# Two 8-byte tiles moved to the right end of SBUF in an FFT filter kernel with a bilinear layer

## The chip, the core and the metric

The kernel runs on one core of a Trainium2 chip. The metric is the device time of one execution in microseconds (us). The core has a matrix engine (TensorE, PE in the profile; PEld is its weight load), VectorE (DVE), ScalarE (ACT), GpSimd (POOL), and queues that issue DMAs (SP's and ACT's are used here). SBUF is the working memory, 128 partitions wide; every tile lies at one byte offset that is the same in all its partitions.

## The reference

```python
X = np.fft.rfft(x, axis=1)                     # x: (8, 3072, 256) float32
Y = X * (filt_r + 1j * filt_i)[None, :, :]     # 1537 x 256 filter
y = np.fft.irfft(Y, n=3072, axis=1).reshape(8 * 3072, 256)
out = ((y @ w_a) * (y @ w_b)) @ w_out          # 256 -> 1536 -> 256, float32 out
```

The weights w_a, w_b and w_out come as float64.

## The kernel before

The transform of length 3072 is done as two stages of matrix products, 128 by 24, forward and inverse (`s1`, `s2`, `is1`, `is2`), with the filter multiplied in between. The bilinear layer follows on each group of 512 rows: `pair` computes two of the twelve column blocks of `y @ w_a` and `y @ w_b` by a seven-product scheme (`term`, lines 582 to 584), multiplies them on VectorE, and `project` (lines 601 to 603) multiplies by `w_out`. Each float32 operand is split in a rounded high part and a low part (`xoh` and `xol`, `gh` and `gl`, `wah` and `wal`, ...), and each product is made of three fp32r matmuls.

Batch 0 is transformed first by functions of its own (`first_s1`, `first_s2`, `first_is1`), in plain float32. During that time and the start of batch 0's layer the float64 weights are converted on VectorE, ScalarE and GpSimd (`conv_...`). From then on the layer of batch b and the transform of batch b + 1 are interleaved by hand: `plan` and `early` hold lists of steps for each slot, and `pair` calls them. The order of instructions on every engine is the order in which the code is written (`manual_schedule`).

SBUF is given out by pools. Those on the left grow upwards in the order `const`, `p2`, then `pw` for the conversion, which is closed and replaced by `later`. Those on the right grow downwards from the end: `fr` for batch 0's transform, which is closed and replaced by `moe`. Each tile takes a multiple of 32 bytes per partition. The offsets of the program before, in bytes, follow from the sizes:

- `const` begins at 1,152. Its first nine tiles (`wah`, `wal`, `wbh`, `wbl`, `woh`, `wol`, `fct`, `flt`, `ict`) have sizes that are multiples of 128, so all nine begin at multiples of 128. `sct` follows at 115,456. It has 8 bytes and takes 32.
- All that lies behind `sct` on the left therefore begins 32 past a multiple of 128: `filt0` to `filt3` and `nyq` in `const`, `xoh`, `xol`, `tt` and `gt` in `p2`, all tiles of `later` (`xt`, `st`, `xh`, `xl`, `zh`, `zl`, `y`, `v`, `yh`, `yl`, `zt`, `t`), and in `pw` `fcf` and `icf`.
- `cut`, again 8 bytes, lies in `pw` behind `icf`; the tiles of `pw` behind it (`raw`, `e`, `m`, `s`) begin 64 past a multiple of 128.
- The right end is at 229,344, which is 96 past a multiple of 128, and all tiles of `fr` and `moe` have sizes that are multiples of 128. So all of them (`x0`, `zf`, `z0`, `xi`; `xf`, `cs`, `g`, `gh`, `gl`, `s`, `ot`, ...) begin 96 past one.

`sct` holds two scale factors for each partition. One DMA (line 699) loads it at 24.6 us, and VectorE reads it in `s2` and `cross` of batches 1 to 7. `cut` holds two constants; two VectorE memsets write it (lines 681 and 682), and the two ScalarE activations of `conv_scale` (lines 260 and 261) read it as their bias.

Of the kernel before, what the change touches and what calls it, by code (L numbers as in the profile page):

```python
# [9 lines left out]
F32 = mybir.dt.float32  # L10
# [186 lines left out]
def fft_filter_bilinear_kernel(ctx: ExitStack, tc, x, filt, fny, wa, wb, wo, s1c, gc, fc, fl, ic, sc, s1f, ff, fi, out):  # L197
# [3 lines left out]
    def pool(name, bufs=1, space=None):  # L201
        kw = {} if space is None else {"space": space}
        return ctx.enter_context(tc.tile_pool(name=name, bufs=bufs, **kw))

    const = pool("const")
    p2 = pool("p2", 2)


    first, front = ExitStack(), ExitStack()
    pw = first.enter_context(tc.tile_pool(name="pw", bufs=1))  # L210
    fr = front.enter_context(tc.tile_pool(name="fr", bufs=2, side="right"))
# [20 lines left out]
    fct = const.tile([128, 3, 128], F32R, name="fct")  # L232
    flt = const.tile([96, 2, 128], F32R, name="flt")
    ict = const.tile([128, 3, 96], F32R, name="ict")
    sct = const.tile([128, 2], F32, name="sct")
    fcf = pw.tile([96, 2, 128], F32, name="fcf")
    icf = pw.tile([128, 2, 96], F32, name="icf")
    cut = pw.tile([128, 2], F32, name="cut")
    filts = [const.tile([128, 2, D], F32, name=f"filt{i}") for i in range(NFT)]
    nyq = const.tile([128, D], F32, name="nyq")  # L240

# [600 lines left out]
```

## Time and profile before

| | before |
|---|---|
| median of 3 runs | 2661.09 us (2660.5 to 2661.87) |
| the profiled execution: its own time | 2662.36 us |
| its span, first to last instruction | 2660.6 us |
| PE busy | 2589.5 us, 97% of the span |
| DVE, ACT, POOL busy | 63%, 53%, 50% |
| granted TensorE clock, mean | 0.985 |
| moved by DMA | 310.88 MB, 117 GB/s over the span |

A share of busy time is a mean over stages. Here there are three: about 200 us in which batch 0 is transformed and the weights are converted, then a steady part to about 2600 us, and an end of some 60 us. "PE busy" counts an instant when at least one matmul is in flight; a matmul's own duration (280 ns) is longer than the distance from one to the next, because they are pipelined.

### The profile page before, as it was taken

The page shows a single profiled execution, that of the slowest core. Times are in us where ns is not written, and L with a number is a line of the kernel's source. Part 1 is how long each engine was busy: PE and PEld are TensorE (multiplying, and loading weights), DVE is VectorE, ACT ScalarE, POOL GpSimd, SP SyncE. Part 2 cuts the span into 40 slices and gives each one's busy share as a digit, 9 for nine tenths or more (in the row PEclk, how much of TensorE's full clock was granted, in tenths as well). Part 3 has the DMA queues.
Part 4 walks back from the last instruction along what each step waited for, and adds up shares of the span by engine and source line. Part 5 has one row for each costly group of instructions (what it writes and reads, how often), then busy time and mean ns, then how long its engine had stood idle before and what let it go on. Part 6 is the DMA issues. An engine that isn't in the chain of part 4 may idle for free.

```text
span 2660.6 us, 54030 instructions
## 1 busy us (share of the span) xinstructions
PE 2589.5 (97%) x20920; PEld 2518.2 (95%) x20920; DVE 1665.2 (63%) x2648; ACT 1412.2 (53%) x2630; POOL 1321.8 (50%) x1044
## 2 busy tenths in 40 slices
PE   5789999999999999999999999999999999999999
PEld 2389999999999999999999999999999999999998
DVE  5775785558845687456865478545884468744443
ACT  3456555555555555555555555555555555545444
POOL 3575454545545555454545545454454545434333
PEclk6899999999999999999999999999999999999999
DMA  7626441344324443244423454234432444311000
GB/s 248 181 98 223 141 135 62 127 150 137 113 74 136 158 137 97 78 163 136 145 66 112 139 154 139 66 119 156 132 120 66 144 152 141 94 33 33 29 21 17
DMA packets 213634, 310.88 MB, mean 117 GB/s; under 512 B 21393, under 2 KB 121298, under 8 KB 213330
## 3 DMA queue, kind: packets, MB, share of 16 engines
q1 hardware_dynamic: 184882, 278.85, 32.7%
q10 hardware_dynamic: 28496, 28.58, 3.5%
q8 instruction: 164, 2.69, 0.4%
q14 instruction: 92, 0.75, 0.1%
HBM read 202.49 MB, written 108.00 MB: 117 GB/s over the span
## 4 chain that ended last, share of the span: by engine, by line
PE 88%; POOL 4%; DVE 3%; issue 2%; DMA 2%; ACT 1%; SPq 0%; ACTq 0%; POOLq 0%; DVEq 0%
PE po L603 10%; PE ps_p L582 10%; PE ps_p L583 9%; PE ps_p L584 9%; PE po L601 9%; PE po L602 9%; PE ps_r L584 5%; PE ps_r L582 5%; PE ps_r L583 5%; PE ps L548 3%; PE ps_q L582 2%; PE ps_q L584 2%; PE ps_q L583 2%; PE ps L361 2%; POOL xol L567 2%
## 5 line engine op out<-in xcount | busy, mean ns | idle before, releaser
L591 POOL TENSOR_TENSOR gl<-g,gh 128x512 fp32r<-128x512 f32 x576 | 747.1, 1297 | 959.2 <-ACT gh L590 894.7
L601 PE MATMUL po<-woh,gh 128*128 128x256 f32 x2304 | 656.1, 285 | 0.0
L603 PE MATMUL po<-woh,gl 128*128 128x256 f32 x2304 | 649.7, 282 | 3.1 <-POOL gl L591 1.1
L590 ACT CAST gh<-g 128x512 fp32r<-128x512 f32 x576 | 358.9, 623 | 550.6 <-DVE g L649 532.0
L602 PE MATMUL po<-wol,gh 128*128 128x256 f32 x2304 | 645.9, 280 | 0.0
L627 DVE TENSOR_TENSOR cs<-ps_r,s 128x512 f32<-128x512 f32 x288 | 199.1, 691 | 450.6 <-PE ps_r L584 397.0
L623 ACT COPY s<-ps_p 128x512 f32<-128x512 f32 x576 | 338.0, 587 | 242.5 <-PE ps_p L584 205.9
L603 PEld LDWEIGHTS po<-woh,gl 128*128 128x128 f32 x2304 | 433.8, 188 | 7.8 <-POOL gl L591 7.8
L601 PEld LDWEIGHTS po<-woh,gh 128*128 128x128 f32 x2304 | 434.9, 189 | 3.1
L602 PEld LDWEIGHTS po<-wol,gh 128*128 128x128 f32 x2304 | 434.7, 189 | 2.9
L582 PE MATMUL ps_p<-xoh,wah 128*128 128x256 f32 x1152 | 326.0, 283 | 12.0 <-DVE cs L627 7.6
L584 PE MATMUL ps_p<-xol,wbh 128*128 128x256 f32 x1152 | 323.9, 281 | 0.0
L583 PE MATMUL ps_p<-xoh,wal 128*128 128x256 f32 x1152 | 323.6, 281 | 0.0
L584 PE MATMUL ps_p<-xol,wah 128*128 128x256 f32 x1152 | 323.1, 280 | 0.0
L582 PE MATMUL ps_p<-xoh,wbh 128*128 128x256 f32 x1152 | 322.7, 280 | 0.0
L583 PE MATMUL ps_p<-xoh,wbl 128*128 128x256 f32 x1152 | 322.6, 280 | 0.0
L627 DVE TENSOR_TENSOR cs<-ps_q,s 128x512 f32<-128x512 f32 x288 | 199.1, 691 | 187.0 <-PE ps_q L584 161.4
L649 DVE TENSOR_TENSOR g<-cs 128x512 f32<-128x512 f32 x288 | 300.9, 1045 | 6.1 <-POOL gl L591 6.1
L567 POOL TENSOR_TENSOR xol<-xf,xoh 128x256 fp32r<-128x256 f32 x192 | 246.9, 1307 | 20.9 <-ACT xoh L566 20.9
L661 DVE TENSOR_TENSOR g<-ps_p,cs 128x256 f32<-128x256 f32 x288 | 122.1, 424 | 213.2 <-ACT cs L660 210.2
L442 POOL TENSOR_TENSOR yl<-y,yh 128x512 fp32r<-128x512 f32 x112 | 144.3, 1289 | 223.7 <-ACT yh L441 223.7
L582 PEld LDWEIGHTS ps_p<-xoh,wah 128*128 128x128 f32 x1152 | 217.5, 189 | 13.8 <-DVE cs L627 8.5
(125 smaller groups left out, 6239.1 us busy)
## 6 DMA issues: line engine op xcount, KB each, us to landing
filt<-in_filt SPq DMA_DIRECT2D x336, 128.0 KB, 2.8
z<-zh SPq DMA_DIRECT2D x112, 256.0 KB, 3.0
zt<-z SPq DMA_DIRECT2D x112, 256.0 KB, 3.0
td<-t ACTq DMA_DIRECT2D x128, 192.0 KB, 2.2
out<-ot SPq DMA_DIRECT2D x95, 256.0 KB, 2.1
tt<-td SPq DMA_DIRECT2D x47, 512.0 KB, 4.2
xt<-in_x SPq DMA_DIRECT2D x84, 256.0 KB, 2.9
st<-s1d SPq DMA_DIRECT2D x84, 256.0 KB, 3.4
```

Of the source, the lines that this page charges most:

```text
L567: nc.gpsimd.tensor_tensor(out=xl[:, o], in0=xf[:, i], in1=f32(xh[:, o]), op=ALU.subtract)
L582: nc.tensor.matmul(o, wh[:, p, w], xh[:, i], start=first and h == 0, stop=False, skip_group_check=True)
L583: nc.tensor.matmul(o, wl[:, p, w], xh[:, i], start=False, stop=False, skip_group_check=True)
L584: nc.tensor.matmul(o, wh[:, p, w], xl[:, i], start=False, stop=True, skip_group_check=True)
L590: nc.scalar.copy(out=gh, in_=g[:, f])
L591: nc.gpsimd.tensor_tensor(out=gl, in0=g[:, f], in1=f32(gh), op=ALU.subtract)
L601: nc.tensor.matmul(o, gh[:, ts], woh[:, n], start=n == 0 and j % 2 == 0, stop=False, skip_group_check=True)
L602: nc.tensor.matmul(o, gh[:, ts], wol[:, n], start=False, stop=False, skip_group_check=True)
L603: nc.tensor.matmul(o, gl[:, ts], woh[:, n], start=False, stop=n == NF - 1, skip_group_check=True)
L623: nc.scalar.copy(out=s, in_=bank)
L627: nc.vector.tensor_tensor(out=cs[:, :, n], in0=bank, in1=s, op=ALU.add)
L649: nc.vector.tensor_tensor(out=g[:, 0].rearrange("p (t n) -> p t n", t=2), in0=cs[:, 0, 0:2], in1=cs[:, 1, 0:2], op=ALU.mult)
```

## The change

A new pool `edge` is opened on the right, ahead of `fr`. It holds one tile `few` of 24 float32 numbers per partition (96 bytes). `sct` becomes its columns 0 and 1, `cut` its columns 2 and 3; the other 20 columns are not used. The two old tiles go. No instruction is added, removed or moved; what changes is the offset at which tiles lie.

```diff
+    edge = ctx.enter_context(tc.tile_pool(name="edge", bufs=1, side="right"))
+    few = edge.tile([128, 24], F32, name="few")
+    sct, cut = few[:, 0:2], few[:, 2:4]
...
     ict = const.tile([128, 3, 96], F32R, name="ict")
-    sct = const.tile([128, 2], F32, name="sct")
     fcf = pw.tile([96, 2, 128], F32, name="fcf")
     icf = pw.tile([128, 2, 96], F32, name="icf")
-    cut = pw.tile([128, 2], F32, name="cut")
     filts = [const.tile([128, 2, D], F32, name=f"filt{i}") for i in range(NFT)]
```

With `few` at 229,248, the right-hand tiles move down by 96 bytes. On the left, what lay behind `sct` moves down by 32, and what lay behind `cut` in `pw` by 64. All of them then begin at multiples of 128.

## Rows read from the trace of the kernel before

**Rows 1.** Busy time by stretch: start:end, length, then each engine, clock, DMA share, GB/s
```profile
0.00:100.00 100.00, 61.36 (x126) 29.62 (x126) 67.86 (x121) 44.02 (x79) 46.28 (x46) 0.74 0.75 241
100.00:200.00 100.00, 78.29 (x478) 66.59 (x479) 68.16 (x117) 49.83 (x99) 61.55 (x54) 0.86 0.34 111
...
300.00:700.00 400.00, 398.99 (x3281) 392.83 (x3279) 272.41 (x414) 217.17 (x403) 202.85 (x158) 1.00 0.40 126
...
1900.00:2300.00 400.00, 399.22 (x3287) 393.43 (x3287) 272.22 (x417) 217.42 (x405) 200.21 (x155) 1.00 0.40 126
...
2600.00:2661.00 61.00, 54.53 (x459) 53.92 (x457) 22.94 (x41) 23.48 (x44) 19.27 (x15) 0.98 0.05 18
```

**Rows 2.** Who waited for whom, 220 to 2600 us: total, times, longest
```profile
PEld po L603 <- POOL gl L591: 6.3, 21, 0.3
...
PEld ps_r L584 <- POOL xol L567: 3.9, 7, 0.6
```

**Rows 3.** Chain that ended last, 0 to 220 us: start, length, what
```profile
3.06 6.72 DMA raw<-in_wa
...
13.53 5.83 DMA z<-z
20.05 4.21 DMA z<-z
...
28.27 5.82 DMA z<-z
...
48.51 6.49 DMA raw<-in_wo
```

**Rows 4.** TensorE's matmuls one by one: start, duration, line, tiles
```profile
1505.42 0.28 PE L601 MATMUL po<-woh,gh 128*128 128x256 f32 x1
...
1506.84 0.28 PE L582 MATMUL ps_p<-xoh,wah 128*128 128x256 f32 x1
...
1507.56 0.28 PE L361 MATMUL ps<-xh,st 128*128 128x256 f32 x1
...
1508.27 0.28 PE L601 MATMUL po<-woh,gh 128*128 128x256 f32 x1
...
1508.98 0.28 PE L582 MATMUL ps_p<-xoh,wah 128*128 128x256 f32 x1
...
1511.79 0.28 PE L601 MATMUL po<-woh,gh 128*128 128x256 f32 x1
...
1512.50 0.28 PE L582 MATMUL ps_r<-xoh,wah 128*128 128x256 f32 x1
```

**Rows 5.** Groups by line and shape on TensorE, 300 to 2500 us
```profile
L603 PE MATMUL po<-woh,gl 128*128 128x256 f32 x2014 | 567.9, 282 | 2.0
...
L584 PE MATMUL ps_p<-xol,wbh 128*128 128x256 f32 x1006 | 282.5, 281 | 0.0
...
L361 PE MATMUL ps<-xh,st 128*128 128x256 f32 x288 | 62.9, 281 | 0.0
...
L407 PE MATMUL ps<-zt,fct 128*128 128x512 f32 x103 | 40.7, 395 | 0.0
```

**Rows 6.** Durations on POOL and ACT by line: ns min/median/max, first and last start
```profile
L285 POOL TENSOR_TENSOR m<-m,e x12: 1257/1266/1474, 14.1 to 170.8; 128x512 f32<-128x512 f32 x12
L514 POOL TENSOR_TENSOR v<-xi,filt x16: 1260/1266/1527, 58.3 to 113.7; 64x512 f32<-64x512 f32 x16
L591 POOL TENSOR_TENSOR gl<-g,gh x576: 1272/1293/1573, 140.6 to 2652.1; 128x512 fp32r<-128x512 f32 x192
L287 ACT CAST woh<-m x6: 612/616/618, 36.2 to 175.5; 128x512 fp32r<-128x512 f32 x6
L590 ACT CAST gh<-g x576: 617/623/634, 139.6 to 2651.4; 128x512 fp32r<-128x512 f32 x192
```

**Rows 7.** What reads the two small tiles, and their load
```profile
L260 ACT ACTIVATE sc<-e,cut x18: 675/688/699, 10.3 to 160.9; 128x512 f32<-128x512 int32 x18
...
L699 SPq DMA_DIRECT2D sct<-in_sc x1: 348/348/348, 24.6 to 24.6; - x1
...
DMA to landing us min/median/max: 1.8/1.8/1.8
```

## The prediction

> **What bounds the kernel now.** I read the busy time by stretch first. From 300 to 2300 us TensorE has a matmul in flight for 399 of every 400 us at full clock, while VectorE works 68% of the time in the two stretches shown and ScalarE and POOL about half [rows 1]. In this part, and it is nearly 2,400 of 2,660 us, the time is the number of matmuls times the distance from one to the next. The first 200 us are different: TensorE is in use for 61 and 78 of 100 us at a granted clock of 0.74 and 0.86, and DMA is at 0.75 of its capacity in the first 100 [rows 1].
>
> Next come the waits of the steady part. TensorE's side waits for POOL to finish a low part, 6.3 us in 21 waits for `gl` and 3.9 us in 7 for `xol` [rows 2]. So everything outside TensorE is worth at most some 10 us there. In the first 220 us the chain shows what ended last; its early links are DMAs, of which the five longest sum to 29.1 us (6.72 + 5.83 + 4.21 + 5.82 + 6.49) [rows 3].
>
> **The change part by part.** It issues the same instructions in the same order, so its cost can only come through addresses or waits.
>
> *The two small tiles themselves.* The 18 + 18 activations that read `cut` take 0.69 us for 512 columns [rows 7]; the bias is one number per partition, and where it lies is 0. The load of `sct` lands 1.8 us after its issue at 24.6 us [rows 7], and nobody reads it before batch 1. One tile now holds both. If waits were kept per tile and not per range of bytes, a read of `cut` behind the load in program order would wait for its landing at 26.4, and the load for the reads ahead of it. The price is bounded by that one landing, under 2 us once, and since the two column ranges don't overlap I take 0.
>
> *TensorE's operands.* This is the term that decides. By the code there are 288 pairs (8 batches, 36 each) with 7 x 6 = 42 matmuls of terms and 24 of the projection, and 84 calls of `s1` with 6: 12,096, 6,912 and 504. Now compare their first bytes modulo 128. In a term the stationary tile (`wah`, ...) is at 0 and the moving one (`xoh`, `xol`) at 32. In the projection it is the other way round: the stationary `gh` or `gl` is at 96, the moving `woh` or `wol` at 0. In `s1` both are at 32. No pair in the kernel has both at 0, as all have after the change, so the price is bounded from these three.
>
> One steady stretch read one by one gives the distances [rows 4]: 24 matmuls of terms from 1508.98 to 1511.79, 2.81 us or 117.1 ns each; 12 of the projection from 1505.42 to 1506.84, 118.3 each; 6 more from 1511.79 to 1512.50, 118.3; 6 of `s1` from 1507.56 to 1508.27, 118.3; but also 6 of a term from 1506.84 to 1507.56, 120.0. The starts are given to 0.01 us, so a run of six is good to 1.7 ns and the run of 24 to 0.4.
>
> - If the lower figure for the terms is due to their aligned stationary tile, the projection and `s1` fall to it: (6,912 + 504) x 1.2 ns = 8.9 us gained.
> - If `s1` is slower than the terms because both its operands are at the same offset modulo 128, then all pairs are so after the change: 12,096 x 1.2 ns = 14.5 us lost.
> - The six of a term at 120.0 in the same stretch have the favourable offsets of a term and are slower than both. The durations in the groups say the same: 282, 281 and 281 ns for the three kinds [rows 5].
>
> I take 0, since runs of one kind differ among themselves (117.1 and 120.0) by more than the kinds do, and keep -8.9 and +14.5 for the range.
>
> Here a rule speaks against this change. The Trainium skill (SBUF — State Buffer, Specifications (TRN2)) gives SBUF lines of 16 bytes. By it a start at 32 or 96 is as much the start of a line as one at 128, and the sum would have 0 here, where the most favourable reading of the rows has -8.9. No row of this trace can show a line's length.
>
> *VectorE, ScalarE, POOL.* A POOL subtraction of 512 columns takes 1266 ns (median) on `m` and `e`, which begin at 64, and 1293 on `g` and `gh`, at 96; a ScalarE cast 616 against 623 [rows 6]. That looks like 1 to 2% for a start that is not a multiple of 64. But POOL's `v` from `xi` and `filt`, at 96 and 32, takes 1266 too [rows 6], and it runs in the first 115 us, as `m` does, while `gl` runs beside a busy TensorE. I take 0. If it were alignment, 27 ns on each of the 28 waits for POOL is 0.8 us; the work behind it is hidden by TensorE.
>
> *DMA.* In the steady part DMA is at 0.40 of its capacity [rows 1], and the waits of that part, from which rows 2 come, hold none of TensorE for a DMA; a cheaper or dearer transfer is hidden. Ahead of 220 us the 29.1 us of chain are open to it [rows 3]. No two transfers there differ by their offset alone. The far bound is the spread between equal ones: `z` is stored in 4.21 us and in 5.83 us, 28% apart, which on 29.1 us is 8.1 us either way. But these stores read from tiles that both begin at 96, so it is the traffic around them that makes the spread, not the address. I take 0.
>
> The Trainium skill (DMA: Bandwidth & Descriptors, How a descriptor splits into AXI transactions) says that a transfer which starts off a multiple of 256 bytes fetches from the multiple below. By that rule a load of 2,048 bytes at 32 past has 65 beats and one at 0 past, where the left tiles come to lie, 64; my estimate from that page is 1.5% of the links, so the sum would be 0.4 us lower. No row here shows beats.
>
> **The sum.** 0 + 0 + 0 + 0 against the profiled execution's span of 2660.6 us. What lies around it is 2662.36 - 2660.6 = 1.8 us and unchanged, and this execution is 1.3 us above the median of the runs, 2661.1. So I predict 2661.
>
> **The rivals.**
>
> *Faster, by aligned operands on TensorE.* The first bullet above: -8.9 us, 2652. For it: the two kinds with a stationary tile off a multiple of 128 both stand at 118.3 in the stretch. Against it: the term at 120.0, and equal durations. Chance 0.22.
>
> *Much faster, by the rate per column.* A matmul of 512 columns lasts 395 ns and one of 256 lasts 281 [rows 5], so a column adds 114 / 256 = 0.445 ns, while a cycle at the granted clock of 1.00, 2.4 GHz, is 0.417. If a column should be one cycle and the rest were a price of misalignment, 256 columns would give back 7 ns, and the 19,512 matmuls above 137 us: 2524. Against it: the moving `woh` is at a multiple of 128 already and no faster. Chance 0.03.
>
> *Slower, by equal offsets.* The second bullet: two operand streams of one matmul that start at the same place modulo 128 get in each other's way. It decides from 0.3 ns per matmul of the terms on (5.3 us over 19,512), and at the 1.2 ns of the rows it is +14.5 us: 2675.6. For it: of the three kinds only `s1` has equal offsets now, and it does not reach the terms' 117.1. Against it: `s1` equals the projection, whose offsets differ. Chance 0.13.
>
> *Hidden anyway.* Engines or transfers do get some per cent faster or slower, and nothing of it shows because TensorE sets the pace: near 2661. This is the same time as the forecast, with another cause. Chance 0.10 of the forecast's total.
>
> **How the numbers follow.** The forecast (no effect, or one that is hidden) has 0.62, the others 0.22, 0.03 and 0.13. A change of 0.2%, 5.3 us, is about what a measurement of this kernel can tell from none; its three runs lie within 1.4 us. So faster is 0.25, same 0.62, slower 0.13. The range reaches from 2648, which takes in the faster case with some margin for a larger distance per matmul, to 2670, which takes in two thirds of the slower one; left out are the large gain and the end of the slower case, and parts of the forecast's tail, under 2 in 10 together. The forecast's own range is 2656 to 2666.
>
> **What would show it.** After the change a run of 24 matmuls of terms should again take 2.81 us and one of 12 of the projection 1.42, and the stretches from 300 to 2300 us should hold as many matmuls as before (3281 and 3287 in the two shown). If the projection's twelve fall to 1.40 and the terms' 24 stay, the first rival is right. If the terms' 24 rise to 2.84, the third is. If the durations of 512 columns fall below 380, the second is. POOL's 1293 ns going to 1266 would show that alignment counts there, with no effect on the end. The prediction would be wrong if TensorE's distance per matmul moved by 0.3 ns or more, or if the chain ahead of 220 us lost or gained a link of 5 us.

## The result and the profile after

The changed kernel takes 2674.91 us (median of 4 runs, 2673.47 to 2676.31) where the kernel before takes 2661.48 (4 runs): ratio 1.0051, 95% interval 1.0033 to 1.0068. It is 13.4 us slower, more than the 5.3 us that the prediction took as the least that can be told from no change, and above its range of 2648 to 2670. The prediction was wrong.

The profiled execution of the changed kernel has a span of 2674.5 us. Its busy time by stretch, in the columns of [rows 1]:

```profile
0.00:100.00 100.00, 60.74 (x126) 29.47 (x126) 67.06 (x120) 43.62 (x78) 46.30 (x46) 0.74 0.72 238
100.00:200.00 100.00, 77.36 (x471) 65.86 (x472) 67.90 (x116) 50.32 (x99) 61.55 (x54) 0.86 0.35 114
...
300.00:700.00 400.00, 399.67 (x3265) 393.57 (x3264) 270.12 (x412) 216.96 (x403) 202.63 (x157) 1.00 0.40 125
...
1900.00:2300.00 400.00, 399.69 (x3269) 393.81 (x3268) 270.37 (x414) 217.07 (x404) 200.23 (x155) 1.00 0.40 126
```

TensorE is in use a little more than before (399.7 of 400 us against 399.0 and 399.2), at the same full clock, and yet holds 3265 and 3269 matmuls where [rows 1] has 3281 and 3287: 0.5% fewer in the same time. 0.52%, the mean of the two stretches, of the 2,460 us behind the first 200 is 12.8 us, nearly the whole loss. Set side by side one by one, the matmuls of the two profiled executions are 0.9 us late at 200 us and 13.9 us late at the end, so 13.0 us are lost behind the first 200. TensorE did not wait more either; these are the waits that answer to [rows 2]:

```profile
PEld po L606 <- POOL gl L594: 4.3, 21, 0.2
PEld ps_r L587 <- POOL xol L570: 3.4, 7, 0.5
```

They fell from 10.2 to 7.7 us. So each matmul takes longer. The stretch of [rows 4] lies here, in the same columns:

```profile
1516.75 0.28 PE L585 MATMUL ps_p<-xoh,wah 128*128 128x256 f32 x1
...
1519.61 0.28 PE L604 MATMUL po<-woh,gh 128*128 128x256 f32 x1
...
1520.32 0.28 PE L585 MATMUL ps_r<-xoh,wah 128*128 128x256 f32 x1
...
1521.75 0.28 PE L604 MATMUL po<-woh,gh 128*128 128x256 f32 x1
...
1523.17 0.28 PE L585 MATMUL ps_p<-xoh,wah 128*128 128x256 f32 x1
```

The first row is the same matmul that started at 1508.98 before [rows 4]; it is 7.8 us late, more than half of the loss at a point somewhat past the middle of the execution. The 24 matmuls of terms behind it take 2.86 us instead of 2.81, the 6 of the projection still 0.71, and 12 more of terms 1.43. Since a row's start is rounded to 0.01 us, the better measure is a mean over the whole steady part. From 300 to 2500 us, the distance between the ends of consecutive matmuls of 256 columns (those above 130 ns, which waited, left out) has these means: terms 117.73 ns before and 118.83 after, over some 10,500 of them in each trace; projection 118.48 and 118.85, over some 6,000.

12,096 x 1.10 ns = 13.3 us for the terms and 6,912 x 0.37 ns = 2.6 us for the projection are 15.9 us; the waits for POOL gave 2.5 back, which leaves 13.4. That is the difference of the medians; the two profiled spans differ by 13.9, so the sum is good to about half a microsecond.

The other engines' instructions did not change. Durations in nanoseconds, min/median/max, which answer to [rows 6]:

```profile
L288 POOL TENSOR_TENSOR m<-m,e x12: 1257/1268/1476, 13.8 to 171.6; 128x512 f32<-128x512 f32 x12
...
L594 POOL TENSOR_TENSOR gl<-g,gh x576: 1273/1290/1571, 141.4 to 2666.1; 128x512 fp32r<-128x512 f32 x192
...
L593 ACT CAST gh<-g x576: 618/622/632, 140.4 to 2665.4; 128x512 fp32r<-128x512 f32 x192
```

### The profile page after: what moved, and what is told of

Same layout as the page of the kernel before. It is cut to its first block, busy times and chain, and to the rows that moved or that the text cites. A ratio compares the mean times of both kernels' runs of the same rounds, so it can differ in the third digit from the quotient of the medians.

```text
span 2674.5 us, 54030 instructions
## 1 busy us (share of the span) xinstructions
PE 2604.4 (97%) x20920; PEld 2533.6 (95%) x20920; DVE 1665.2 (62%) x2648; ACT 1412.9 (53%) x2630; POOL 1321.3 (49%) x1044
## 4 chain that ended last, share of the span: by engine, by line
PE 93%; DVE 2%; DMA 1%; POOL 1%; issue 1%; ACT 1%; SPq 0%; ACTq 0%; POOLq 0%; DVEq 0%
PE po L606 10%; PE ps_p L585 10%; PE po L604 10%; PE ps_p L586 10%; PE ps_p L587 10%; PE po L605 10%; PE ps_r L587 5%; PE ps_r L586 5%; PE ps_r L585 5%; PE ps L551 3%; PE ps_q L585 3%; PE ps_q L587 2%; PE ps_q L586 2%; PE ps L364 2%; PE ps L411 2%; PE ps L410 2%
```

## The experiments

In all of them nothing but the places of tiles is changed (e12 also joins the six weights in one tile). An unused tile in front of the weights (`pad_w`) or behind `ict` (`pad_l`) moves what follows on the left, and the size of `few` moves all on the right. The difference in the table is the byte offset of a matmul's moving tile minus that of its stationary one, modulo 256, first for the terms, then for the projection. It is worked out from the sizes in the code and the two ends of SBUF; no trace holds an address. The distances are means as defined above, over some 10,500 and 6,000 matmuls of each run's profile.

| run | what is where | difference, terms / projection | distance, ns: terms / projection | median, us |
|---|---|---|---|---|
| before | | 160 / 160 | 117.73 / 118.48 | 2661.5 |
| after | | 128 / 0 | 118.83 / 118.85 | 2674.9 |
| e1_all_at_32 | all of after, weights too, 32 further | 128 / 0 | 118.83 / 118.85 | 2675.6 |
| e2_left_at_32 | after, left at 32 | 160 / 0 | 117.73 / 119.19 | 2668.0 |
| e3_right_at_96 | after, right at 96 | 128 / 32 | 118.75 / 116.92 | 2661.8 |
| e4_left_on_128 | after, left 128 further | 0 / 0 | 119.82 / 119.95 | 2694.0 |
| e5_both_32 | | 32 / 32 | 117.06 / 117.12 | 2647.7 |
| e6_both_96 | | 96 / 96 | 120.17 / 118.66 | 2689.6 |
| e7_both_192 | | 192 / 192 | 115.84 / 117.62 | 2637.7 |
| e8_both_224 | | 224 / 224 | 118.37 / 118.30 | 2669.4 |
| e9_weights_only | after, weights alone moved | 192 / 192 | 115.87 / 117.63 | 2637.5 |
| e10_192_and_32 | | 192 / 32 | 116.48 / 116.85 | 2642.7 |
| e11_both_64 | | 64 / 64 | 117.73 / 117.80 | 2660.5 |
| e12_weights_16_more | e9, weights 16 further | 176 / 208 | 118.72 / 118.09 | 2668.9 |

The medians of before beside these runs were 2661.5 to 2661.9.

**All 32 further.** The weights begin 32 bytes later, and everything else with them:

```diff
+    const.tile([128, 8], F32, name="pad_w")
     wah = const.tile([128, NP, 7, 128], F32R, name="wah")
...
-    few = edge.tile([128, 24], F32, name="few")
+    few = edge.tile([128, 16], F32, name="few")
```

> All tiles, the weights too, begin 32 past a multiple of 128; so the two operands of every matmul have equal offsets, as in the changed kernel, but none begins at a multiple of 128. Theory A (equal offsets of a matmul's stationary and moving tile cost about 1 ns each): about 2675 us, as the changed kernel. Theory B (what costs is a start at a multiple of 128 itself): about 2661 us. Theory C (no law of 128; any move of a tile moves the time): somewhere else.

2675.56 us, ratio to before 1.0050 (1.0035 to 1.0065), and the two mean distances equal the changed kernel's to 0.01 ns. So it is not a start at a multiple of 128 that costs, and theory B falls. A common shift of all tiles by 32 bytes changes nothing; what this run leaves is the tiles' places relative to one another.

**The left as before, and the right near where it was.** The first adds `const.tile([128, 8], F32, name="pad_l")` behind `ict`, the second makes `few` 32 columns wide.

> The weights at 0, the tiles behind them on the left (xoh, xol, st, zt, yh ...) at 32 as in the kernel before, the right ones (gh, gl, cs ...) at 0 as in the changed one. Theory A: the terms are as before, so 12,096 x 1.1 ns = 13 us come back, and the projection keeps its 0.45 ns x 6,912 = 3 us: 2662 to 2665 us. Theory B: the same. A theory that the right ones (the engines that write them) make the difference: about 2675 us.

> The left at 0 as in the changed kernel, the right at 96 as in the kernel before: the other half. Theories A and B: only the projection's 3 us come back, 2672 us, and the terms' 24 matmuls stay at the changed kernel's distance. A theory that the right ones make the difference: 2661 us.

The left at 32 has 2667.95 us (ratio 1.0023, 1.0014 to 1.0033): the terms are back at 117.73 ns exactly, while the projection did not keep its 118.85 and is the slowest of these three at 119.19. So the time is 3 us above the 2662 to 2665 of theories A and B. The right at 96 has 2661.79 us (1.0000, 0.9991 to 1.0009). Here theory A missed by 10 us: the terms stay slow, as it said, but the projection falls to 116.92 ns, well below what it had before, although modulo 128 its offsets are those of before. One stretch of it, each row the first of a kind:

```profile
1507.97 0.28 PE L585 MATMUL ps_p<-xoh,wah 128*128 128x256 f32 x1
...
1510.81 0.28 PE L604 MATMUL po<-woh,gh 128*128 128x256 f32 x1
...
1512.93 0.28 PE L604 MATMUL po<-woh,gh 128*128 128x256 f32 x1
...
1514.33 0.28 PE L585 MATMUL ps_p<-xoh,wah 128*128 128x256 f32 x1
```

24 matmuls of terms take 2.84 us here, 12 of the projection 1.40 (1.42 in the changed kernel). By the means, the projection follows the move of its own tiles (118.85 to 116.92 ns) and the terms, whose tiles stayed, hardly change (118.83 to 118.75). And 128 is not the period.

**The left 128 further.** `const.tile([128, 32], F32, name="pad_l")`; all offsets modulo 128 are those of the changed kernel.

> The changed kernel, with all tiles behind the weights on the left moved up by 128 bytes: the offsets modulo 128 are the same, those modulo 256 are not. Theory A with a period of 128 or less: 2675 us. Theory C: any other time.

2694.03 us, ratio 1.0120 (1.0105 to 1.0135), 19 us above the changed kernel. Theory A is gone. The stretch of 24 matmuls of terms:

```profile
1524.06 0.28 PE L586 MATMUL ps_p<-xoh,wah 128*128 128x256 f32 x1
1524.18 0.28 PE L587 MATMUL ps_p<-xoh,wal 128*128 128x256 f32 x1
1524.30 0.28 PE L588 MATMUL ps_p<-xol,wah 128*128 128x256 f32 x1
...
1526.94 0.28 PE L605 MATMUL po<-woh,gh 128*128 128x256 f32 x1
```

Every step is 0.12, and the 24 take 2.88 us: 120.0 ns each, as if on a grid. So I formed theory D: what counts is the difference of a matmul's two offsets, modulo 256.

**The other multiples of 32.** The sizes of `pad_l` and `few` in columns of four bytes:

```diff
-    few = edge.tile([128, 24], F32, name="few")
+    few = edge.tile([128, 32], F32, name="few")    # both 32;  96: 48, 192: 8, 224: 16, 64: 40
...
+    const.tile([128, 40], F32, name="pad_l")       # both 32;  96: 56, 192: 16, 224: 24, 64: 48
```

> Theory D: what counts is the moving tile's offset minus the stationary one's, modulo 256. So far 160 (terms before), 128 (terms after), 0 (terms with the left moved by 128; projection after) and 32 (projection with the right at 96) have shown 117.7, 118.8, 119.8 and 118.9, and 116.9 ns from one matmul to the next. Here terms and projection both have 32. D: both near 116.9 ns, so 12,096 x 0.8 + 6,912 x 1.6 = 21 us less than before, 2640 us. Rival A (period of 128, equal offsets cost): a difference of 32 is that of the kernel before, 2661 us. Rival C (no law in the difference): no better than 2655 us.

> Difference 96 modulo 256 for terms and projection, not seen so far. D: both kinds move to one common distance, within 0.5 ns of one another, whatever it is. C: they differ by more than 1 ns.

> Difference 192 for both. D: one common distance, within 0.5 ns. If only equality modulo 128 cost (A), 192 would be as 160: 2661 us or less.

> Difference 224 for both. D: one common distance, within 0.5 ns. A: as before, 2661 us or less.

At 32 both kinds came to 117.1 ns, as D said, and to 2647.72 us (0.9946, 0.9931 to 0.9961): faster than before, but 8 us short of its figure. The means fell by 0.67 and 1.36 ns, which is 17.5 us and not 21, and the waits for POOL grew from 10.2 to 12.0 us; where the rest of the 8 lies stays open. At 224 the kinds came to 118.4 and 118.3, and to 2669.35 us (1.0027, 1.0016 to 1.0037), where theory A had 2661 or less. At 96 (2689.56 us, 1.0103, 1.0088 to 1.0118) and 192 (2637.74 us, 0.9909, 0.9892 to 0.9925) the kinds lie 1.5 and 1.8 ns apart, at 96 as theory C had said. So D in the form "one common distance" missed twice out of four; a difference sets a kind's distance, but not the same for both kinds.

**The weights alone.** The six weights and the tables `fct`, `flt` and `ict` between the two pads move by 192 bytes; in the steady part TensorE alone reads these, though ScalarE and POOL write them in the first part. All other tiles keep their offsets modulo 256:

```diff
+    const.tile([128, 48], F32, name="pad_w")
     wah = const.tile([128, NP, 7, 128], F32R, name="wah")
...
+    const.tile([128, 16], F32, name="pad_l")
     filts = [const.tile([128, 2, D], F32, name=f"filt{i}") for i in range(NFT)]
```

> The changed kernel with the weights alone moved (to 64 past a multiple of 256); all tiles that ScalarE, VectorE, POOL and the DMAs use keep their offsets modulo 256. The difference moving minus stationary becomes 192 for terms and projection, as in the run with both at 192. Theory D (the relation between TensorE's two operands alone sets it): 2638 us, the terms at 115.8 ns and the projection at 117.6. Rival E (the offsets of the other tiles, against the engines that write them or the DMAs that load them): as the changed kernel, 2675 us.

2637.46 us, ratio 0.9912 (0.9897 to 0.9926), and 115.87 and 117.63 ns, those of the run at 192 to 0.03 ns. The distance between the projection's two tiles differs by exactly 256 bytes between these two runs, and its 117.6 ns does not, which fits a period of 256. Its stretches, and what TensorE waits for:

```profile
300.00:700.00 400.00, 398.41 (x3307) 392.31 (x3308) 275.44 (x419) 219.39 (x408) 203.12 (x158) 1.00 0.40 127
1900.00:2300.00 400.00, 398.36 (x3312) 392.37 (x3311) 276.07 (x419) 220.72 (x410) 207.81 (x161) 1.00 0.38 121
```

```profile
PEld po L608 <- POOL gl L596: 9.4, 21, 0.5
...
PEld ps_r L589 <- POOL xol L572: 4.3, 7, 0.6
```

3307 and 3312 matmuls in 400 us, 42 and 43 more than the changed kernel, and less of TensorE's time in use than in any row of [rows 1] from that part: it is so fast now that the waits for POOL grow to 13.7 us. Theory E falls in the form that was put: the tiles of the other engines and DMAs begin where they did modulo 256, and the time is 37 us less. But modulo 256 this run is the one at 192 with every tile 64 bytes lower, so it repeats that run and the common shift of e1. What no run holds apart is the place of the weights against TensorE's other operand and against the accesses of the other engines and DMAs on the same side. The traces do. Among the terms during which POOL, ScalarE and VectorE are all idle (from 120 ns before a matmul's start to its end, some 150 in each trace) the mean distance is 117.2 ns before, 118.2 in the changed kernel, 120.0 with the left 128 further and 114.6 here. Among those with no DMA packet under way (from 300 ns ahead of the matmul in front, some 3,200) it is 117.8, 118.7, 119.8 and 115.2. The differences stay where that traffic is absent, so they do not come from it, and TensorE's own accesses are left.

**Mixed, and the last two values.** e10 has `pad_l` of 16 columns and `few` of 32. e12 holds the six weights in one tile, from which they are cut 16 bytes later.

> Terms at a difference of 192, where they were 115.8 ns, and the projection at 32, where it was 116.9 to 117.1. D, with the two kinds independent of one another: 0.6 ns x 6,912 = 4 us less than the run with both at 192, 2634 us. If they are not independent: 2638 us or more.

2642.66 us (0.9929, 0.9915 to 0.9944), 9 us above the figure for independent kinds and in the range for the other case: the projection is at its good 116.85 ns, but the terms, whose tiles lie as in the run at 192, are at 116.48 instead of 115.84. The two kinds are not independent. The projection at a difference of 0 shows it as well: 118.85, 119.19 and 119.95 ns beside terms at 128, 160 and 0. The traces hold a third case. The two tiles of `s1` lie in one pool at a difference of 0 in every run, and yet its mean over 432 matmuls goes from 117.6 ns (both at 96) to 120.0 (both at 64). With its own tiles at the same places modulo 256 it is 119.2 in the changed kernel and 118.5 in e12. So a matmul's own difference does not settle its distance; what lies around it counts too.

> Difference 64 for both, the last multiple of 32 not seen. If a difference and the one 128 further are alike (32 and 160 were 117.1 and 117.7 for terms, 0 and 128 were 119.8 and 118.8): near the run at 192, 2638 to 2650 us. If the period is 256 with no such kinship: anywhere up to 2690 us.

2660.53 us (0.9996, 0.9986 to 1.0006), no kin of 192: the period is not 128 here either.

> As the run with the weights alone moved, but with them 16 bytes further, so that the difference is 176 for terms and 208 for the projection. If the distance per matmul changes evenly between multiples of 32: terms 116.8 ns (between 117.7 at 160 and 115.8 at 192), projection 118.0, about 2652 us. If only steps of 32 count: one of the neighbours, 2638 or 2661 us.

2668.86 us (1.0026, 1.0015 to 1.0037). At 176 the terms have 118.72 ns, more than at 160 and at 192. Neither forecast held: the distance does not change evenly, and steps below 32 count too.

## Why the prediction was wrong

**TensorE's operands: the step that failed.** The prediction took 0 for this term, "since runs of one kind differ among themselves (117.1 and 120.0) by more than the kinds do". It measured +13.3 us for the terms and +2.6 for the projection. Per matmul that is 1.10 and 0.37 ns, both beyond the 0.3 that the prediction had named as a sign of its being wrong. Two things were wrong in that step. Each of the three kinds of [rows 4] occurs in that trace at one pair of places only, so no row could show what another pair does to it; likeness between different kinds was taken for proof that places don't matter. And six matmuls whose starts are rounded were set against twenty-four, where the trace holds thousands of each; their means would have shown real differences of 0.7 ns between the kinds.

**The slower rival had the figure and not the cause.** It said 2675.6 for equal offsets modulo 128. The measured 2674.9 is close by chance. It is made of 13.3 and 2.6 less 2.5 of waits, where the rival had 14.5 for the terms alone; and equality modulo 128 is neither needed (the terms at a difference of 96 are the slowest of all, 120.17 ns) nor what sets the size (0 and 128 are equal modulo 128 and differ by 1.0 ns). The prediction let it decide from 0.3 ns on, but spread the 5.3 us over all 19,512 matmuls; over the 12,096 of the terms, which alone this rival slows, it is 0.44 ns. The first rival, that an aligned stationary tile speeds TensorE up, is refuted by the result: the projection, whose stationary tile now begins at a multiple of 128, went from 118.48 to 118.85 ns. So is the second, a large gain per column: 256 columns did not get 7 ns faster in any run.

**The rules.** The Trainium skill (SBUF — State Buffer, Specifications (TRN2)) gives 16-byte lines, by which all these starts are equal; the runs differ by 57 us, so that rule is not enough. The Trainium skill (TensorE: Matmul & The Clock Gate, Step-by-step: what each phase is for) gives TensorE two independent read ports and says that loading the next weights doesn't take read bandwidth from the running matmul. If the two reads had no influence on one another, one would not expect the relation of their places to count; over these runs the distance goes from 115.8 to 120.2 ns, and the measurement decides. That it is these two reads which disturb each other is not shown.

**The two small tiles: right.** No wait for the joint tile appears among TensorE's, and the first 200 us hold nearly the same work (126 and 471 matmuls against 126 and 478). The 0.9 us by which the matmuls are late at 200 us lies within what the other profiled executions show there (1.0 us early to 1.5 late).

**VectorE, ScalarE, POOL: right.** On POOL and ScalarE 1290 ns against 1293 and 622 against 623, now that all starts are multiples of 128; on VectorE the sums `cs` take a mean of 691 ns in both. POOL's `m` keeps 1268 against 1266 as well, so the 1 to 2% of [rows 6] are not the start modulo 128. That they are the stage, as the prediction held, is likely and was not tried alone.

**DMA: right, though its sign of being wrong showed.** DMA is at 0.72 and 0.35 of capacity in the first two stretches against 0.75 and 0.34, and a packet of 2,048 bytes takes a median of 84 ns in both traces. The prediction would have been wrong too if the chain ahead of 220 us lost or gained a link of 5 us, and it did both: `raw<-in_wo` of 6.49 us is no longer on it, and this is:

```profile
49.54 6.61 DMA zf<-z
```

The two nearly cancel, so the sign was badly chosen: a link can change its name at almost no cost.

**Open.** Why one difference is better than another is not settled. That a matmul's moving tile is read while the next stationary one is loaded might explain it, but no run holds these two reads apart. The influence of one kind on the other (e10) and the spread of `s1` say that more than one difference counts. A start at other multiples of 4 or 16 was not tried beyond e12.

## What to carry to other kernels

When TensorE is in use all the time, as here, the bytes at which its two operands begin can be worth up to 2%: 2637 to 2694 us for one and the same list of instructions. Alignment to a round number was no guide in this kernel. Take the count of matmuls in a fixed stretch, or the mean distance over thousands of them, and try pads of 32 to 224 bytes between the tiles that TensorE reads together. A pad ahead of the weights alone moves all that lies behind them along, as in e1, so it needs a second one behind them: 192 bytes ahead and 64 behind made this kernel 0.9% faster than the version before and 1.4% faster than the changed one. And an edit that moves tiles can change the time by this much with no other cause, so compare edits with the places held fixed.

## What the runs showed of the hardware

The distance from one fp32r matmul of 256 columns to the next depends on the places of tiles relative to one another: on the difference between the byte offsets of its own moving and stationary tiles, and on more than that (e10, `s1`). For the terms, by the difference modulo 256: 119.8 ns at 0, 117.1 at 32, 117.7 at 64, 120.2 at 96, 118.8 at 128, 117.7 at 160, 118.7 at 176, 115.8 at 192 (116.5 with the projection at 32), 118.4 at 224. The same difference gives another distance to another kind: at 96 the projection has 118.7, at 192 it has 117.6. Moving all tiles together by 32 (e1) changes the terms and the projection by less than 0.01 ns, and by 64 (the two runs at 192) by at most 0.03; two differences that are 128 apart give the terms distances that are 0.7 to 1.9 ns apart. POOL, ScalarE and the DMAs showed no such change when their tiles moved from 32, 64 or 96 past a multiple of 128 to 0 (1293 to 1290 ns, 623 to 622, and 84 ns for a packet of 2,048 bytes in both).
